# Retention and a Mish feed-forward layer on one core: the opening and the second block in another order

## The chip, the cores and the metric

The kernel runs on one core of one Trainium2 chip. The core has five engines with a queue of instructions each: TensorE (PE, with the loads of its stationary operand shown as PEld), VectorE (DVE), ScalarE (ACT), GpSimd (POOL) and SyncE (SP, which here only starts DMAs). They run side by side and wait for one another by semaphores. Matmuls write to PSUM, eight banks of 2 KB on each of 128 partitions; everything else lies in SBUF. The metric is the time of one execution on the device, in microseconds (us); lower is better.

## The reference

Two stages follow each other. The first is a recurrence over 768 positions for 4 batches and 8 heads of 64 elements, with one decay per head. Its output, 3072 rows of 512, goes through a two-layer feed-forward net whose middle is h * tanh(softplus(h)), the Mish function.

```python
batch, n_heads, seq, head_dim = (4, 8, 768, 64)
n_tokens, d_model, d_ff = (3072, 512, 2048)
for t in range(S):
    state = gamma[None, :, None, None] * state + np.einsum('bhd,bhe->bhde', k[:, :, t], v[:, :, t])
    y[:, :, t] = scale * np.einsum('bhd,bhde->bhe', q[:, :, t], state)
...
h = x @ w_in
sp = np.where(h > 20.0, h, np.log1p(np.exp(np.minimum(h, 20.0))))
g = h * np.tanh(sp)
return (g @ w_out).astype(np.float32)
```

## The kernel before

**The recurrence by chunks.** Positions are taken in 24 chunks of 128 (six to a batch). For a chunk the recurrence becomes matmuls: scores (k turned, times q turned), a triangular mask, the "present" product (masked scores times v), the outer product of k and v that updates the state, and the "past" product (the state before, times q). The decay is folded into q, k and v by tables (`qvs`) when they are cast to 16-bit floats. Two neighbouring chunks make a pair, numbered `n`; inside a pair, `m` is the first or second half of the positions, `a` the first or second four heads. For pairs 0 to 2 the functions are `cast_pair` (scale and cast), `turn_pair` (four transposes by TensorE into a PSUM tile `t_ps`, then a copy to SBUF), `pair_scores` (16 matmuls into a PSUM tile `at`, then one mask operation on DVE that gives `am`), `pair_outer` (into `u_ps`), `pair_state` (for m = 0 the middle state `mid`, for m = 1 `suh` and `sth`), `pair_present` and `pair_past` (both into `y_ps`) and `pair_xt` (copies y to `xt`, the input of the feed-forward net). Before `pair_past` adds to a y that `pair_present` has written, ScalarE copies one column of it to `seen`.

**The feed-forward net by blocks.** The first block is four chunks (512 rows), the others are two (256 rows). In a block, `g1` (line 560) multiplies weights with xt into `h_ps`, and ACT applies Mish (line 568). For block 0 a unit u of `g1` is four matmuls of 512 columns, 16 units in all; then come 16 units of the second layer (`g2_mm`, line 574), four matmuls each, the last two arranged so that output tiles end one after the other. The weights arrive as 32-bit floats in four slices for each layer, through staging tiles (`wstage`, four buffers), and are cast to 16 bit by `cast_win` (line 169, two halves to a slice, on DVE) and `cast_wout`. Later blocks do the second layer with seven products instead of eight (`seven`, line 660); nothing there is touched.

**The order.** It is written out by hand: within an engine the instructions run in the order in which the program issues them (`manual_schedule`). The function `first_block` (line 735) issues all loads on SP's queue in the order q, k, v of the first four chunks, first-layer weights, second-layer weights, the third pair; then it walks through the opening, lines 745 to 809. A dictionary `plan` (line 827) hangs further steps behind units of block 0: the casts of the second layer's weights, `turn_two` behind unit 24, the scores of pair 2 behind 25 and 26, `outer_two` behind 28 and `y_two` behind 30, which makes the input of block 1.

**PSUM.** Three tiles of a bank (`mm`), one of a bank (`px`) and two of two banks (`at`) share the eight banks, each group in rotation; a new tile waits until the readers of the one that it replaces are done. Two engines that access one PSUM tile are ordered by the program, also where they access different banks of it: in `turn_two`, the second eight transposes wait for the copy of the first eight, and of the two y in one tile the second is copied after the first.

**Identity matmuls.** `spin(n)` (line 378) multiplies the identity with itself, n times 128 columns, four at a time in one matmul of 512 columns, into a score tile that is overwritten afterwards. Its output is not used; it keeps TensorE busy where it would wait.

Of the kernel before, what the change touches and what calls it, by code (L numbers as in the profile page):

```python
# [10 lines left out]
FP32 = mybir.dt.float32  # L11
# [5 lines left out]
def kernel(  # L17
# [145 lines left out]

    def cast_win(s):
        src = wtmps.pop(("in", s))
        wins[s] = []
        for j in range(2):
            t = cpool.tile([P, NBP, TB // 2], FP16, name=f"win{s}_{j}")
            nc.vector.tensor_copy(t, src[:, :, j * (TB // 2):(j + 1) * (TB // 2)])
            wins[s].append(t)  # L170
# [27 lines left out]
    def turn_parts(parts, dst, on_act=False):  # L198
        t_ps = mmps.tile(list(dst.shape), FP16, name="t_ps", tag="mm")
        turn_into(parts, dst, t_ps, on_act)  # L200

    def turn_into(parts, dst, t_ps, on_act):
        for i in range(dst.shape[1]):
            for r in range(dst.shape[2]):
                nc.tensor.transpose(t_ps[:, i, r], parts(i, r), ident)  # L205
        if on_act:
            nc.scalar.copy(dst, t_ps)  # L207
        else:
            nc.vector.tensor_copy(dst, t_ps)
# [96 lines left out]
    def pair_state(n, u, m):  # L306
        g = 2 * n + m
        if m == 0:
            st = stp.tile([P, HP, D], FP16, name="mid")
            if n == 0:  # L310
                nc.vector.tensor_copy(st, u[0])
            else:
                nc.vector.tensor_tensor(st, u[0], states[g - 1], op=ALU.add)
# [63 lines left out]

    def spin(n):
        at = pairs[min(k for k in pairs if type(k) is tuple and k[1] == "at")]
        to = at.rearrange("p h i r c -> p h (i r) c")  # L380
        for i in range(0, n, HP):
            m = min(HP, n - i)
            nc.tensor.matmul(  # L383
                to[:, 0, :m], ident, ident.unsqueeze(1).broadcast_to((P, m, P)),
                start=True, stop=True)
# [349 lines left out]
    def first_block():  # L735
# [8 lines left out]

        pair_at(0, 0)
        spin(50)
        turn_first_q(qf, 0, True)
        spin(14)
        turn_first_q(qf, 1, False)
# [9 lines left out]
        turn_pair(0, "k", 0, True)  # L759
        spin(6)  # L760
        pair_scores(0, 0)
        pair_at(0, 1)
        spin(2)
        turn_pair(0, "k", 1, True)
        spin(6)
        pair_scores(0, 1)
        pair_at(1, 0)
        spin(2)
        turn_pair(1, "k", 0, True)
        spin(4)  # L770
# [36 lines left out]
        pair_state(1, u, 1)  # L807
# [11 lines left out]
        def turn_two():  # L819
            t_ps = atps.tile([P, 2, HP, 2, C], FP16, name="t_ps", tag="at")  # L820
            for j, nm in enumerate("qk"):
                pairs[2, nm + "t"] = qktp.tile([P, HP, 2, C], FP16, name="qkt", bufs=6)
                turn_into(
                    lambda i, r: pairs[2, nm, i // 2][:, r, i % 2 * 2:i % 2 * 2 + 2],
                    pairs[2, nm + "t"], t_ps[:, j], nm == "k")

# [34 lines left out]

    def banks(name, width):
        t = atps.tile([P, 2, TB], FP32, name=name, tag="at")
        return [t[:, m, :HP * width].rearrange("p (i c) -> p i c", i=HP) for m in range(2)]

    def outer_two():
        u = banks("u_ps", D)[:1]
        for a in range(2):
            pair_outer(2, u, a)
        pair_state(2, u, 0)  # L870

    def y_two():
        y = banks("y_ps", C)
        for a in range(2):
            pair_present(2, y, a)
        for m in range(2):
            nc.scalar.copy(seen, y[m][:, 0, :1])
# [120 lines left out]
```

## Time and profile before

| | |
|---|---|
| median of 3 runs | 212.36 us (210.85 to 212.54) |
| the profiled execution | 211.39 us, its span 209.6 us |
| mean granted TensorE clock | 0.984 |
| busy, share of the span | PE 94%, PEld 71%, DVE 52%, ACT 43%, POOL 35% |
| PE instructions | 2794 matmuls, 2794 weight loads |
| DMA | 38.75 MB, mean 185 GB/s |

Times in rows are counted from the first instruction of the span. A group of instructions is written as line, engine, operation, output <- inputs by the program's names, shapes and count, then busy time and the mean of one in ns, then the idle time of the engine just before and what ended it. A row of the timeline has start and length ahead of that. The chain is the work that ended last, followed back from the end; "issue" is time in which an engine waited for nothing that the profile shows. Line numbers are those of the kernel before.

### The profile page before, as it was taken

The numbers are of one execution on the slowest core, as the hardware profiler recorded it, in microseconds if no ns is written. First come the engines' busy times: TensorE is split into PE (matmuls) and PEld (weight loads), VectorE is DVE, ScalarE is ACT, GpSimd is POOL, SyncE is SP. The second block draws the span as 40 slices with busy tenths as digits, with TensorE's granted clock in tenths as the row PEclk, the third lists the DMA queues.
The fourth block names the chain that finished last, engine by engine and source line by source line (L and its number), as shares of the span: only waits on it lengthen the run. The fifth ranks groups of instructions, "written<-read, shape, count | busy, mean of one in ns | idle before, by whom it ended". The sixth has DMA issues, their size and how long they took to land.

```text
span 209.6 us, 6381 instructions
## 1 busy us (share of the span) xinstructions
PE 196.3 (94%) x2794; PEld 149.8 (71%) x2794; DVE 108.2 (52%) x195; ACT 89.7 (43%) x163; POOL 72.5 (35%) x91
## 2 busy tenths in 40 slices
PE   7973799998999999999999999999999999999994
PEld 2542244443486588888888888888788888888883
DVE  0583854005396445928765565745735734645062
ACT  2372266531154155254255254363364463452640
POOL 5550000738570500486551921913904800000000
PEclk9999599999999999999999999999999999999999
DMA  6999999999999995069999999999891430200202
GB/s 188 297 319 366 281 368 339 330 233 211 219 243 243 230 155 119 0 145 244 216 169 271 217 181 266 187 169 272 136 217 43 87 117 3 103 0 5 100 25 78
DMA packets 92828, 38.75 MB, mean 185 GB/s; under 512 B 76160, under 2 KB 86912, under 8 KB 92800
## 3 DMA queue, kind: packets, MB, share of 16 engines
q1 hardware_dynamic: 92656, 38.28, 82.5%
q8 instruction: 22, 0.36, 0.7%
q10 hardware_dynamic: 144, 0.05, 0.1%
q14 instruction: 6, 0.05, 0.1%
HBM read 27.32 MB, written 6.29 MB: 160 GB/s over the span
## 4 chain that ended last, share of the span: by engine, by line
PE 88%; ACT 4%; DMA 3%; issue 2%; DVE 1%; POOL 1%; SPq 0%; POOLq 0%; ACTq 0%; DVEq 0%
PE h_ps L560 41%; PE o_ps L660 27%; PE o_ps L574 9%; PE y_ps L493 4%; DMA kf<-in_k_dram 3%; ACT qkt L207 2%; PE at L405 1%; PE u_ps L412 1%; PE t_ps L205 1%; ACT xt L351 1%; PE y_ps L336 1%; PE at L282 1%; ACT v L248 1%; POOL qk L250 1%; PE y_ps L327 1%
## 5 line engine op out<-in xcount | busy, mean ns | idle before, releaser
L560 PE MATMUL h_ps<-xt,win 128*128 128x256 f16 (+1 forms) x704 | 88.3, 286 | 1.9 <-ACT xt L351 1.7
L560 PEld LDWEIGHTS <-win 128*128 128x128 f16 x704 | 68.9, 99 | 19.1 <-issue 3.6
L568 ACT ACTIVATE g<-h_ps 128x512 f16<-128x512 f32 x96 | 57.3, 597 | 50.9 <-PE h_ps L560 50.9
L660 PEld LDWEIGHTS <-gsum 128*128 128x128 f16 x288 | 27.0, 98 | 3.8 <-DVE gsum L638 0.4
L660 PE MATMUL o_ps<-tmat,gsum 128*128 128x256 f16 x216 | 26.4, 273 | 0.0
L360 POOL TENSOR_TENSOR qk<-qf,qvs 128x512 f16<-128x512 f32 x18 | 19.1, 1064 | 14.7 <-DMA qf<-in_q_dram 6.2
L660 PEld LDWEIGHTS <-g 128*128 128x128 f16 x216 | 21.1, 98 | 2.5
L574 PE MATMUL o_ps<-wout,g 128*128 128x512 f16 x96 | 22.4, 380 | 0.0
L364 POOL TENSOR_TENSOR v<-vf,qvs 128x512 f16<-128x512 f32 x18 | 20.6, 1145 | 1.6 <-DMA vf<-in_v_dram 1.5
L629 DVE TENSOR_TENSOR gsum<-g 128x512 f16<-128x512 f16 x18 | 7.9, 439 | 25.6 <-ACT g L568 25.6
L362 POOL TENSOR_TENSOR qk<-kf,qvs 128x512 f16<-128x512 f32 x18 | 20.3, 1125 | 0.2
L666 ACT COPY snap<-o_ps 128x256 f32<-128x256 f32 x27 | 10.1, 373 | 19.4 <-PE o_ps L660 19.4
L901 POOL COPY summed<-gsum 128x1 f16<-128x1 f16 x6 | 1.1, 188 | 48.6 <-DVE gsum L634 29.2
L660 PE MATMUL o_ps<-wout,g 128*128 128x256 f16 x144 | 17.2, 273 | 0.0
L674 DVE TENSOR_TENSOR osb<-o_ps,snap 128x256 f32<-128x256 f32 x27 | 11.4, 424 | 10.3 <-PE o_ps L660 5.9
L574 PEld LDWEIGHTS <-g 128*128 128x128 f16 x96 | 8.8, 98 | 9.7
L547 ACT CAST xt<-y_ps 128x512 f16<-128x512 f32 x13 | 7.2, 588 | 13.5 <-PE y_ps L493 13.5
L449 DVE TENSOR_TENSOR mid<-u_ps,sth 128x256 f16<-128x256 f32 x15 | 6.3, 422 | 11.3 <-PE u_ps L412 11.0
L482 DVE TENSOR_TENSOR am<-at,tri_half 128x1024 f16<-128x1024 f32 x9 | 10.9, 1214 | 0.0
L383 PE MATMUL at<-ident 128*128 128x512 f16 (+1 forms) x26 | 8.9, 470 | 1.4 <-POOL ident L96 1.4
L250 POOL TENSOR_TENSOR qk<-qf,qvs 128x512 f16<-128x512 f32 x2 | 2.1, 1076 | 23.0 <-PE h_ps L560 23.0
L660 PE MATMUL o_ps<-wout,gsum 128*128 128x256 f16 x72 | 9.4, 273 | 0.0
(77 smaller groups left out, 182.4 us busy)
## 6 DMA issues: line engine op xcount, KB each, us to landing
kf<-in_k_dram SPq DMA_DIRECT2D x24, 256.0 KB, 5.6
vf<-in_v_dram SPq DMA_DIRECT2D x24, 256.0 KB, 5.4
out_dram<-osb SPq DMA_DIRECT2D x22, 256.0 KB, 3.2
qf<-in_q_dram SPq DMA_DIRECT2D x20, 256.0 KB, 5.0
wt<-in_moe_w_out_dram SPq DMA_DIRECT2D x3, 1024.0 KB, 7.2
wi<-in_moe_w_in_dram SPq DMA_DIRECT2D x4, 512.0 KB, 7.7
wi<-in_moe_w_in_dram SPq DMA_DIRECT2D x2, 1024.0 KB, 11.2
qfirst<-in_q_dram SPq DMA_DIRECT2D x2, 512.0 KB, 4.5
```

Of the source, the lines that this page charges most:

```text
L360: nc.gpsimd.tensor_tensor(q16, qf, qs[g % 2].unsqueeze(2).broadcast_to((P, H, D)), op=ALU.mult)
L362: nc.gpsimd.tensor_tensor(k16, kf, boosts.unsqueeze(2).broadcast_to((P, H, D)), op=ALU.mult)
L364: nc.gpsimd.tensor_tensor(v16, vf, vs[g % 2].unsqueeze(2).broadcast_to((P, H, D)), op=ALU.mult)
L383: nc.tensor.matmul(to[:, 0, :m], ident, ident.unsqueeze(1).broadcast_to((P, m, P)), start=True, stop=True)
L482: nc.vector.tensor_tensor(am.rearrange("p a j i c -> p (a j i) c"), at.rearrange("p a j i c -> p (a j i) c"), tri_half.unsqueeze(1).broadc ...
L493: nc.tensor.matmul(ys[blk][s][half(hh), j, i], w, x, start=key not in begun, stop=True, skip_group_check=True)
L560: nc.tensor.matmul(h_ps[:, j], wins[s][f // 2][:, bp, f % 2 * P:(f % 2 + 1) * P], xts[blk][:, bp, :nt], start=(bp == 0), stop=(bp == NBP - 1))
L568: nc.scalar.activation(gt, h_ps, AF.Mish, scale=inv_boost3)
L574: nc.tensor.matmul(o_ps, gts[blk, fb][:, t * P:(t + 1) * P], wouts[s][:, f, cols], start=(fb == 0), stop=(fb == NFB - 1))
L660: nc.tensor.matmul(o_ps, x(f), w(f), start=first and f == 0, stop=f == n - 1, skip_group_check=True)
L666: nc.scalar.copy(x, o_ps)
L674: nc.vector.tensor_tensor(dst, o_ps, plus, op=ALU.add)
```

## The change

In the opening:

- The identity matmuls at its start and around the turns of pair 0 are issued with 128 columns each instead of 512 (`per=1`), 46, 14, 8 and 8 of them; the shorter runs after a new score tile go. Two of 512 and one of 512 columns stay ahead of the scores of pair 1.
- Both turns of pair 1 come ahead of its scores. The scaling of v stands behind these turns, and the outer product of pair 0 is split: four heads ahead of the last scores, four behind.
- The first middle state is copied by ACT instead of DVE. The second state of pair 0 is made behind its present product, and the outer product of pair 1 stands between present and past of pair 0.
- The y of pair 1 is two tiles of one bank (`mm`) instead of one tile of two banks (`at`). The copy of pair 0's second y is issued behind the `seen` copies of pair 1.
- The first half of the first weight slice is cast by POOL, ahead of the last two copies of y, instead of by DVE behind them.

At the end of block 0: `turn_two` makes all 16 transposes and then both copies on DVE; the present product of pair 2 gets a step of its own, one unit earlier than the past product; its y is two tiles, the first copied by DVE, the second by ACT.

```diff
-    def cast_win(s):
+    def cast_win(s, first_on=None):
...
-            nc.vector.tensor_copy(t, src[:, :, j * (TB // 2):(j + 1) * (TB // 2)])
+            (j == 0 and first_on or nc.vector).tensor_copy(
+                t, src[:, :, j * (TB // 2):(j + 1) * (TB // 2)])
...
     def turn_parts(parts, dst, on_act=False):
         t_ps = mmps.tile(list(dst.shape), FP16, name="t_ps", tag="mm")
-        turn_into(parts, dst, t_ps, on_act)
+        turn_only(parts, t_ps)
+        taken(dst, t_ps, on_act)
...
             if n == 0:
-                nc.vector.tensor_copy(st, u[0])
+                nc.scalar.copy(st, u[0])
...
-    def spin(n):
+    def spin(n, per=HP):
...
-        for i in range(0, n, HP):
-            m = min(HP, n - i)
+        for i in range(0, n, per):
+            m = min(per, n - i)
...
         pair_at(0, 0)
-        spin(50)
+        spin(46, 1)
         turn_first_q(qf, 0, True)
-        spin(14)
+        spin(14, 1)
         turn_first_q(qf, 1, False)
...
         turn_pair(0, "k", 0, True)
-        spin(6)
+        spin(8, 1)
         pair_scores(0, 0)
         pair_at(0, 1)
-        spin(2)
         turn_pair(0, "k", 1, True)
-        spin(6)
+        spin(8, 1)
         pair_scores(0, 1)
-        pair_at(1, 0)
-        spin(2)
         turn_pair(1, "k", 0, True)
-        spin(4)
         cast_pair(0, "v", 0)
-        pair_scores(1, 0)
-        pair_at(1, 1)
-        spin(2)
         turn_pair(1, "k", 1, True)
         for n, a in ((0, 1), (1, 0), (1, 1)):
             cast_pair(n, "v", a)
+        pair_at(1, 0)
+        spin(8)
+        pair_scores(1, 0)
+        u = [mmps.tile([P, HP, D], FP32, name="u_ps", tag="mm") for _ in range(2)]
+        pair_outer(0, u, 0)
+        pair_at(1, 1)
         spin(4)
         pair_scores(1, 1)
-        u = [mmps.tile([P, HP, D], FP32, name="u_ps", tag="mm") for _ in range(2)]
-        for a in range(2):
-            pair_outer(0, u, a)
-        for m in range(2):
-            pair_state(0, u, m)
+        pair_outer(0, u, 1)
+        pair_state(0, u, 0)
...
             pair_present(0, y, a)
+        nc.scalar.copy(seen, y[1][:, 0, :1])
         pair_xt(0, y, 0)
-        nc.scalar.copy(seen, y[1][:, 0, :1])
-        pair_past(0, y, 1)
-        pair_xt(0, y, 1)
-        u = banks("u_ps", D)
+        pair_state(0, u, 1)
+        u = u_banks()
         for a in range(2):
             pair_outer(1, u, a)
+        pair_past(0, y, 1)
         pair_state(1, u, 0)
-        y = banks("y_ps", C)
+        z = [mmps.tile([P, HP, C], FP32, name="y_ps", tag="mm") for _ in range(2)]
         for a in range(2):
-            pair_present(1, y, a)
+            pair_present(1, z, a)
         for m in range(2):
-            nc.scalar.copy(seen, y[m][:, 0, :1])
-        pair_past(1, y, 0)
-        pair_past(1, y, 1)
-        pair_xt(1, y, 0, False)
-        pair_xt(1, y, 1)
-        cast_win(0)
+            nc.scalar.copy(seen, z[m][:, 0, :1])
+        pair_xt(0, y, 1)
+        for m in range(2):
+            pair_past(1, z, m)
+        cast_win(0, nc.gpsimd)
+        pair_xt(1, z, 0, False)
+        pair_xt(1, z, 1)
         pair_state(1, u, 1)
...
             for j, nm in enumerate("qk"):
+                turn_only(
+                    lambda i, r: pairs[2, nm, i // 2][:, r, i % 2 * 2:i % 2 * 2 + 2], t_ps[:, j])
+            for j, nm in enumerate("qk"):
                 pairs[2, nm + "t"] = qktp.tile([P, HP, 2, C], FP16, name="qkt", bufs=6)
...
+                taken(pairs[2, nm + "t"], t_ps[:, j], False)
...
             29: [(outer_two,)],
+            30: [(present_two,)],
             31: [(y_two,)],
...
-    def y_two():
-        y = banks("y_ps", C)
+    def present_two():
+        y = pairs["y"] = [
+            atps.tile([P, HP, C], FP32, name="y_ps", tag="at") for _ in range(2)]
...
+    def y_two():
+        y = pairs["y"]
         for m in range(2):
             pair_past(2, y, m)
         for m in range(2):
-            pair_xt(2, y, m)
+            pair_xt(2, y, m, m == 1)
```

More of the change, by code (lines that the diff above doesn't have):

```diff
@@ L199, in turn_parts, with turn_only, taken @@
         t_ps = mmps.tile(list(dst.shape), FP16, name="t_ps", tag="mm")
-        turn_into(parts, dst, t_ps, on_act)
-    def turn_into(parts, dst, t_ps, on_act):
-        for i in range(dst.shape[1]):
-            for r in range(dst.shape[2]):
+        turn_only(parts, t_ps)
+        taken(dst, t_ps, on_act)
+    def turn_only(parts, t_ps):
+        for i in range(t_ps.shape[1]):
+            for r in range(t_ps.shape[2]):
                 nc.tensor.transpose(t_ps[:, i, r], parts(i, r), ident)
+    def taken(dst, t_ps, on_act):
         if on_act:
@@ L376, in cast_to @@
             ncast[0] += 1
-    def spin(n):
-        at = pairs[min(k for k in pairs if type(k) is tuple and k[1] == "at")]
+    def spin(n, per=HP):
+        at = pairs[min(x for x in pairs if type(x) is tuple and x[1] == "at")]
         to = at.rearrange("p h i r c -> p h (i r) c")
-        for i in range(0, n, HP):
-            m = min(HP, n - i)
+        for i in range(0, n, per):
+            m = min(per, n - i)
             nc.tensor.matmul(
@@ L821, in turn_two @@
             for j, nm in enumerate("qk"):
+                turn_only(
+                    lambda i, r: pairs[2, nm, i // 2][:, r, i % 2 * 2:i % 2 * 2 + 2], t_ps[:, j])
+            for j, nm in enumerate("qk"):
                 pairs[2, nm + "t"] = qktp.tile([P, HP, 2, C], FP16, name="qkt", bufs=6)
-                turn_into(
-                    lambda i, r: pairs[2, nm, i // 2][:, r, i % 2 * 2:i % 2 * 2 + 2],
-                    pairs[2, nm + "t"], t_ps[:, j], nm == "k")
+                taken(pairs[2, nm + "t"], t_ps[:, j], False)
         plan = {
@@ L860, in first_block, with u_banks @@
                 fn(*args)
-    def banks(name, width):
-        t = atps.tile([P, 2, TB], FP32, name=name, tag="at")
-        return [t[:, m, :HP * width].rearrange("p (i c) -> p i c", i=HP) for m in range(2)]
+    def u_banks():
+        t = atps.tile([P, 2, TB], FP32, name="u_ps", tag="at")
+        return [t[:, m, :HP * D].rearrange("p (i c) -> p i c", i=HP) for m in range(2)]
     def outer_two():
-        u = banks("u_ps", D)[:1]
+        u = u_banks()[:1]
         for a in range(2):
```

## The prediction

> **What bounds the kernel now.** I read the page first, then the chain that ended last in order of time over the first 60 us, then the busy times of the engines in 3.41 us windows with the granted clock.
>
> ```profile
> PE 88%; ACT 4%; DMA 3%; issue 2%; DVE 1%; POOL 1%; SPq 0%; POOLq 0%; ACTq 0%; DVEq 0%
> ```
>
> PE sets the time, so only stretches where PE stands still or runs slowly on this chain are worth anything. The chain shows them all in the opening and at the end of the first block:
>
> ```profile
> 16.94 2.36 issue
> 19.31 0.22 PE u_ps L300 x3
> ...
> 21.65 0.70 DVE xt L353
> 22.35 0.02 issue
> 22.37 0.59 ACT xt L351
> 22.97 0.04 issue
> 23.01 15.94 PE h_ps L560 x64
> 38.95 7.77 PE o_ps L574 x36
> ```
>
> (Start, length, what.) Two losses stand here. One is 2.36 us at 16.94 in the middle of an outer product whose last three matmuls wait for no data. The other is hidden in a busy row: 64 first-layer matmuls take 15.94 us, 0.249 each, while the 36 of the same width behind them take 7.77, 0.216 each. At 0.216 the 64 would take 13.8.
>
> The windows (length, busy of PE, PEld, DVE, ACT, POOL with counts, then granted clock, DMA share, GB/s) say why:
>
> ```profile
> 0.00:16.94 16.94, 13.04 (x223) 7.12 (x224) 8.93 (x11) 7.66 (x14) 8.87 (x27) 1.00 0.99 274
> 13.37:16.78 3.41, 2.15 (x121) 1.59 (x119) 2.98 (x4) 2.71 (x7) 0.17 (x1) 1.00 1.12 353
> 16.78:20.19 3.41, 0.83 (x52) 0.58 (x39) 0.85 (x2) 0.67 (x2) 0.00 (x0) 1.00 1.06 363
> 20.19:23.60 3.41, 1.65 (x18) 1.10 (x18) 1.95 (x4) 0.79 (x3) 0.00 (x0) 0.50 1.06 388
> 23.60:27.01 3.41, 3.41 (x10) 1.21 (x8) 3.38 (x7) 0.98 (x2) 0.00 (x0) 0.50 0.81 222
> 204.51:207.92 3.41, 1.96 (x18) 1.51 (x16) 1.27 (x3) 0.00 (x0) 0.00 (x0) 1.00 0.28 92
> q8 instruction: 22, 0.36, 0.7%
> q8 instruction: 1, 0.02, 5.7%
> ```
>
> A window with PE busy for 0.83 of 3.41 us (24%), the one with the stop, is followed by half clock. It goes on through one of 48% and ends with one that is full. Windows at 63% and 57% (the first row with a length of 3.41 and the last) cost no clock. The two lines below are the DMA queue of code, first over the whole span, then between 16.5 and 17.7 us: one packet of 0.02 MB, the first of this queue in the span. It lands inside the stop, and 223 + 224 = 447 PE instructions lie before the stop. So I read the stop as PE out of code: the first 447 were there, the next block came late because the DMA share is 0.99 up to there.
>
> **The change, part by part.** I laid out the new order instruction by instruction with the durations of these rows (groups have busy time and mean ns, timeline rows start and length; the line on landing is that of `wi`):
>
> ```profile
> 7.39 4.15 POOL L250 TENSOR_TENSOR qk<-kf,qvs 128x512 f16<-128x512 f32 x4 [3.33 <-DMA kf<-in_k_dram]
> L207 ACT COPY qkt<-t_ps 128x512 f16<-128x512 f16 x4 | 2.3, 586 | 3.0 <-PE t_ps L205 3.0
> L666 ACT COPY snap<-o_ps 128x256 f32<-128x256 f32 x27 | 10.1, 373 | 19.4 <-PE o_ps L660 19.4
> L209 DVE COPY qkt<-t_ps 128x1024 f16<-128x1024 f16 x2 | 1.4, 691 | 11.4 <-PE t_ps L205 11.4
> 24.25 3.69 DVE L169 CAST win<-wi 128x1024 f16<-128x1024 f32 x6
> 9.01 6.00 SPq L152 DMA_DIRECT2D wi<-in_moe_w_in_dram  x6
> DMA to landing us min/median/max: 6.0/8.8/11.2
> L318 DVE TENSOR_TENSOR sth<-suh,gch 128x256 f16<-128x256 f32 x2 | 0.8, 424 | 0.1
> 9.61 0.42 PE L282 MATMUL at<-qkt 64*64 64x128 f16 x16 [0.35 <-ACT qkt L207]
> 12.68 0.42 PE L282 MATMUL at<-qkt 64*64 64x128 f16 x16 [0.46 <-ACT qkt L207]
> 14.05 1.67 ACT L248 ACTIVATE v<-vf 128x512 f16<-128x512 f32 x3
> ```
>
> *Shorter identity matmuls.* 26 matmuls become 79 of nearly the same columns (90 to 88 times 128). No time is saved: the chain here runs over the landing of k (POOL waits 3.3 us for it). But each is two PE instructions, so the opening has 106 instructions more, and 176 stand before the first scores instead of 78. PE's code is fetched by blocks: 22 packets move 0.36 MB, about 16 KB, or 256 instructions each, by the 5588 instructions of PE and PEld. If the late block is asked for one block ahead, that is at instruction 447 - 256 = 191: before, in the third scores, at 12.68; after (counting two per matmul) in the first scores, at 9.61. The latency was 19.31 - 12.68 = 6.6 us, so the code is there at 16.2. PE then comes to instruction 447 in the middle of the first "present" product, at 14.6. The stop is 1.6 us instead of 2.36. Bounds: no stop at all (a fetch 1.6 us faster), and, if what is queued ahead on the DMA sets the landing and not the request, 17.8: the first weight load, issued before the request, lands at 9.0 + 6.0 = 15.0 (row above), and PE went on at most 19.31 - 16.5 = 2.8 after the code packet began.
>
> *Turns ahead of scores, v behind the turns.* The fourth k cast still ends at 11.5. ACT now runs copy, v, copy and then the three v casts from 11.8: 0.59 + 0.56 + 0.59 + 1.67 = 15.2, where it ended at 15.7 before. The first mid moves from DVE to ACT's end (0.37, by the snap row), so the state chain on DVE begins at 15.5 and ends at 16.5, 0.7 earlier. DVE's masks end before that.
>
> *Outer between present and past, y in two tiles.* After the code arrives at 16.2: rest of present 0 and outer 1 to 17.2 (16 and 32 matmuls by the 0.42 for 16 of the score rows, readable 0.2 later), mid 17.7, present 1 to 17.85, two reads of `seen` to 18.25, the past products to 18.5. Before, DVE's copy of the first y waited for both past products and ACT's for DVE's copy (0.70, then 0.59 in the chain), since both halves were one tile. As two tiles they run side by side; but ACT has also the delayed copy of y 1 (0.59) ahead of its own, so it ends at 18.25 + 0.59 + 0.59 = 19.4. DVE: the second half of the first weight slice at 17.7 (3.69 / 6, 0.62), then its copy, 18.5 to 19.2. The first layer starts at **19.45** instead of 23.01: **3.55 us**.
>
> *The first weight cast on POOL.* The rows hold no POOL cast of 128x1024. Bounds: DVE's 0.62, and twice POOL's two-input 128x512 (4.15 / 4), 2.1; I take 2.1, the same engine. The weight lands at 15.0; POOL has done its masks by then, so the cast ends at 17.1, two us ahead of its use. Behind it on POOL stand only the casts of the second block, whose loads come much later. SP is the other side: its first second-layer load waits for both casts of this slice and is now released some five us earlier, but on the DMA, full then, it stands behind the first-layer loads. Nothing of this is counted.
>
> POOL's cast runs beside DVE's `sth`. What two such do to each other shows here, both started near 59 us:
>
> ```profile
> 58.92 0.68 DVE L613 TENSOR_TENSOR tmat<-wout 128x1024 f16<-128x1024 f16 x1
> 59.64 1.42 DVE L614 TENSOR_TENSOR tmat<-wout,tmat 128x1024 f16<-128x1024 f16 x1
> 59.08 1.43 POOL L360 TENSOR_TENSOR qk<-qf,qvs 128x512 f16<-128x512 f32 x1 [2.21 <-DMA qf<-in_q_dram]
> ```
>
> The same DVE shape takes 0.68 alone and 1.42 beside POOL, and POOL 1.43 instead of 1.04. So `sth` could end at 17.55 instead of 16.5. With the stop at 16.2 the `seen` reads at 18.25 cover this, and DVE is 0.25 later, 19.45, level with ACT. Without the stop it would cost 0.9. The Trainium skill, "SBUF — State Buffer", section "SBUF: two separate sides", says of the port pair that VectorE and GpSimd share that a VectorE operation with two SBUF inputs and a GpSimd read lock each other out for a whole instruction. By that rule the loss is as just worked out, and the rows agree.
>
> *Clock.* With the start at 19.45 PE's poorest 3.41 us has, by this layout, some 1.7 to 1.9 us busy (49% to 56%). Kept were 57% and 63%, lost 24%. I take it as kept: 64 matmuls at 0.216, 13.8 instead of 15.94, **2.1 us**. The Trainium skill, "TensorE: Matmul & The Clock Gate", Part 1 (The HAM clock gate), gives an activity window of about 3.4 us and half rate after an idle one; the 6.8 us at 0.50 are two such windows, though here a window 24% busy sufficed.
>
> *Second block.* PE's own rows:
>
> ```profile
> 47.95 0.61 PE L205 MATMUL t_ps<-ident,qk 128*128 128x128 f16 x8 [0.78 <-DVE qkt L209]
> 49.66 0.42 PE L282 MATMUL at<-qkt 64*64 64x128 f16 x16 [0.24 <-ACT qkt L207]
> 56.51 0.41 PE L336 MATMUL y_ps<-qkt,sth 64*64 64x128 f16 x8 [0.51 <-ACT seen L877]
> 58.30 1.91 PE L560 MATMUL h_ps<-xt,win 128*128 128x256 f16 x16 [0.19 <-ACT xt L351]
> ```
>
> 1.72 us of idleness. Sixteen transposes in a row remove the 0.78, but both copies (0.69 each on DVE) then follow them, and only four matmuls lie beside: about 0.8 idle at the scores instead of 1.02. The `seen` wait (0.51) falls under four matmuls. DVE, however, must first finish two output copies (128x512 from PSUM, as the 0.70 of its xt) before its copy of y, so the next block waits some 0.5 instead of 0.19. Together **0.4 us**, between 0 and 1.2.
>
> *What is late next.* PE would now come six us earlier to all that the DMA brings:
>
> ```profile
> 29.22 1.23 DVE L179 CAST wout<-wt 128x2048 f16<-128x2048 f32 x1 [1.27 <-DMA wt<-in_moe_w_out_dram]
> 39.48 1.14 ACT L248 ACTIVATE qk<-kf 128x512 f16<-128x512 f32 x2
> 43.72 1.05 ACT L177 CAST wout<-wt 128x1024 f16<-128x1024 f32 x1 [0.46 <-DMA wt<-in_moe_w_out_dram]
> ```
>
> Even at these old times all are ready. The third weight slice (the third and fourth of the six casts from 24.25) is half cast by 26.1 and needed at 19.45 + 32 x 0.216 = 26.4; the second layer's first by 30.5, needed at 33.2; k of the second block by 40.6, needed at 41.0; the last quarter by 44.8, needed at 48. Two margins are under half a us, so a start earlier than 19.45 gains little more.
>
> **The sum**: 3.55 + 2.1 + 0.4 = 6.05 us. The profiled execution took 211.39 (span 209.6 and 1.79 around it), so 205.3 for it; the median of the runs is 0.97 above that execution, so **206.3** beside 212.36.
>
> **Rivals.** *The clock halves all the same* (25%). For it: 49% to 56% lies under the lowest share seen kept, and the window's phase may differ. Half clock from about 17 us to 23.6 costs 0.5 in the products and half of 3.6 in the first layer, 2.3: 208.6. To 27 us it costs 4: 210.3.
>
> *The code comes no earlier than the DMA lets it* (10%). All loads issued up to the request are served first; then it is there at 17.8, the start is 1.6 later, 21.05, and the clock falls as before: 1.95 + 0.4, 210.0.
>
> *The stop is not code* (5%), and 2.4 us of it stay, with the half clock: without the 1.6 at present 0 the start is near 20.9, gain 2.1 + 0.4, 209.9. Against it stand the packet inside the stop and the absence of a wait. The Trainium skill, "Runtime: NRT & Kernel Launch", section Instruction fetch mechanics, says so in effect: 16 KiB blocks, whose fetch is mostly hidden, and room for 2048 instructions on PE. The block size agrees with the trace; the hiding and the room do not, with a stop at 447.
>
> *Slower* (8%): POOL's cast, and DVE locked beside it. Its place is between 15.0 and the first layer; nothing else can supply that weight. It decides once it ends after about 23 us, that is when it lasts over 8 us, four times my price, because PE then idles and loses its clock as well. At 10 us the first layer starts at 25.05 and loses 1.7 more by half clock: 40.6 at its end instead of 38.95, less 0.4: 213.6.
>
> **How the numbers follow.** 52% for the forecast, which spreads from 204 (no stop: one us more at most) to 208 (the second block gives nothing, or the stop is a us longer). With the halved clock and half of the two 210 cases, the range is 204 to 210.3. Faster by over 1% (about what a measurement here can tell from no change) means under 210.2: 80%; within 1%: 12%, from the ends of the 210 cases; slower: 8%.
>
> **What would show it.** Right: first h_ps at 19 to 20 us; an "issue" row of 1 to 2 us inside L327's group instead of L300's; no 0.50 in the windows; no wait of ACT xt for DVE xt. Wrong: granted clock of 0.50 between 17 and 27; POOL's weight cast over 4 us; PE waiting for DVE win or wout past 25 us; a second code stop some 25 matmuls into the first layer.

## The result and the profile after

The changed kernel takes 204.13 us (median of four, 203.94 to 206.89) beside 211.84 us for the kernel before (median of four, 210.85 to 212.54). The ratio is 0.967, with a 95% interval of 0.958 to 0.976. The forecast was 206.3 us.

The profiled execution took 203.98 us with a span of 202.2 and a mean TensorE clock of 0.998. The chain that ended last, of the kernel after, in order of time (start, length, what), for the stretch that the prediction is about:

```profile
7.89 6.96 DMA vf<-in_v_dram
...
14.87 0.64 ACT v L252
...
17.17 0.65 PE y_ps L340 x16
...
17.84 0.59 ACT xt L355
...
18.48 0.69 DVE xt L357
19.18 0.14 issue
19.32 13.97 PE h_ps L564 x64
33.29 7.77 PE o_ps L578 x36
...
41.99 1.30 DVE qkt L213 x2
...
43.33 0.42 PE at L286 x16
...
50.34 0.97 PE o_ps L578 x4
...
51.33 3.77 PE h_ps L564 x33
```

Three things are to be seen. The first layer starts at 19.32 where it started at 23.01, and the row of 2.36 us of "issue" has no successor: the longest such row here is 0.14. The 64 matmuls of the first layer take 13.97 instead of 15.94. From their end to the next block's first matmul there are 18.04 us (33.29 to 51.33) instead of 19.35 (38.95 to 58.30). What the chain starts from is new as well: the load of v, which landed at 14.85.

The windows of 3.41 us of the kernel after (length; busy of PE, PEld, DVE, ACT, POOL with counts; granted clock, DMA share, GB/s) are laid from the first change of clock in the trace (6.96 us), so that a change falls on an edge. They keep full clock through the poorest one, in which PE is busy for 1.91 us, 56%:

```profile
17.20:20.62 3.42, 1.91 (x23) 1.07 (x23) 2.73 (x6) 1.43 (x4) 0.45 (x1) 1.00 1.08 369
20.62:24.03 3.41, 3.41 (x17) 1.54 (x16) 1.23 (x2) 2.35 (x5) 0.00 (x0) 1.00 1.05 387
```

The timeline of the same execution shows who releases whom ahead of the first layer and at the end of the block (start, length, engine and line, idle time before and what ended it):

```profile
14.87 0.63 ACT L252 ACTIVATE v<-vf 128x512 f16<-128x512 f32 x1 [0.43 <-DMA vf<-in_v_dram]
16.47 1.18 POOL L169 CAST win<-wi 128x1024 f16<-128x1024 f32 x1 [2.94 <-DMA wi<-in_moe_w_in_dram]
16.32 0.43 DVE L322 TENSOR_TENSOR sth<-suh,gch 128x256 f16<-128x256 f32 x1
17.88 0.69 DVE L169 CAST win<-wi 128x1024 f16<-128x1024 f32 x1 [0.60 <-DMA wi<-in_moe_w_in_dram]
49.39 1.29 DVE L587 COPY osb<-o_ps 128x512 f32<-128x512 f32 x2 [1.65 <-PE o_ps L578]
50.38 0.58 ACT L355 CAST xt<-y_ps 128x512 f16<-128x512 f32 x1 [1.13 <-PE y_ps L340]
50.59 0.68 DVE L357 CAST xt<-y_ps 128x512 f16<-128x512 f32 x1
```

Three engines wait for the DMA here, which they did not do before: ACT for the last v, POOL for the first half of the weight slice (landed near 16.4, before at 15.0), DVE for the second half (near 17.85). The code queue carried its first packet early, as the DMA view of the kernel after between 11.8 and 13.1 us shows:

```profile
q8 instruction: 1, 0.02, 5.8%
```

The packet runs from 11.82 to 13.04; before, from 16.59 to 17.68. Where the 7.41 us between the two profiled executions (211.39 and 203.98) came from:

| place | before | after | gain | forecast |
|---|---|---|---|---|
| first layer starts | 23.01 | 19.32 | 3.69 | 3.55 |
| its 64 matmuls | 15.94 | 13.97 | 1.97 | 2.1 |
| from there to the next block | 19.35 | 18.04 | 1.31 | 0.4 |
| the rest | | | 0.44 | 0 |

The rest lies behind the start of the next block and is not followed further.

### The profile page after: what moved, and what is told of

The parts are those of the page before. It is cut to its first block, busy times and chain, and to the rows that moved or that the text cites. A ratio compares the mean times of both kernels' runs of the same rounds, so it can differ in the third digit from the quotient of the medians.

```text
span 202.2 us, 6489 instructions
## 1 busy us (share of the span) xinstructions
PE 194.1 (96%) x2847; PEld 153.3 (76%) x2847; DVE 110.0 (54%) x195; ACT 88.6 (44%) x162; POOL 73.4 (36%) x92
## 4 chain that ended last, share of the span: by engine, by line
PE 89%; DMA 3%; SPq 3%; DVE 1%; ACT 1%; issue 0%
PE h_ps L564 42%; PE o_ps L664 28%; PE o_ps L578 10%; PE y_ps L497 4%; DMA vf<-in_v_dram 3%; SPq L236 3%; PE at L409 1%; PE u_ps L416 1%; PE y_ps L340 1%; DVE qkt L213 1%; PE y_ps L331 1%; SPq L194 0%; PE t_ps L207 0%; PE at L286 0%; DVE xt L357 0%
## 5 line engine op out<-in xcount | busy, mean ns | idle before, releaser
L564 PE MATMUL h_ps<-xt,win 128*128 128x256 f16 (+1 forms) x704 | 86.2, 282 | 1.5 <-DVE xt L357 1.5
L364 POOL TENSOR_TENSOR qk<-qf,qvs 128x512 f16<-128x512 f32 x18 | 18.7, 1041 | 17.4 <-DMA qf<-in_q_dram 17.4
L387 PE MATMUL at<-ident 128*128 128x128 f16 (+1 forms) x79 | 8.2, 278 | 1.4 <-POOL ident L96 1.4
L664 PE MATMUL o_ps<-tmat,g 128*128 128x256 f16 x72 | 9.3, 273 | 0.0
```

The costliest lines, as they stand in the source:

```text
L364: nc.gpsimd.tensor_tensor(q16, qf, qs[g % 2].unsqueeze(2).broadcast_to((P, H, D)), op=ALU.mult)
L387: nc.tensor.matmul(to[:, 0, :m], ident, ident.unsqueeze(1).broadcast_to((P, m, P)), start=True, stop=True)
L564: nc.tensor.matmul(h_ps[:, j], wins[s][f // 2][:, bp, f % 2 * P:(f % 2 + 1) * P], xts[blk][:, bp, :nt], start=(bp == 0), stop=(bp == NBP - 1))
L664: nc.tensor.matmul(o_ps, x(f), w(f), start=first and f == 0, stop=f == n - 1, skip_group_check=True)
```

## The experiments

The theory after the result: the narrow identity matmuls bring the first code block about five us earlier, so the stop goes, and with it the half clock; the rest of the opening, and the second block apart from it, give about two us. The rival: the new order of the opening did it, and the width of the identity matmuls is of no account. Each ratio is to the kernel before on the same chip.

### The new order with wide identity matmuls

```diff
-        spin(46, 1)
+        spin(46)
...
-        spin(14, 1)
+        spin(14)
...
-        spin(8, 1)
+        spin(8)
...
-        spin(8, 1)
+        spin(8)
```

> The changed kernel with its identity matmuls 512 columns wide again (46, 14, 8 and 8 times 128 columns as before, in matmuls of up to 512), all else as changed. Theory 'code': the late block of PE code is asked for some 4 us later, its packet comes at 15.5 to 17 us instead of 11.8, PE stops for 1.5 to 3 us at the second present product, the clock falls to 0.50 behind it, the first layer starts at 21 to 22 us; 3 to 5 us slower than the changed kernel, 207 to 209. Rival 'order': the new order of turns, scores and products removed the stop; then within 0.5 us of the changed kernel, about 204. Second expectation of 'code': the load under way when the packet runs is the one that lands late; so the last v lands at 13.5 again instead of 14.85, and the first weight at 15.0.

Measured: 210.0 us (209.31 to 210.81), ratio to the kernel before 0.989 [0.985, 0.993]. The chain of this kernel has the stop again, and longer:

```profile
15.71 0.41 PE y_ps L340 x8
16.13 3.44 issue
19.56 0.69 PE y_ps L331 x32
...
22.24 16.36 PE h_ps L564 x64
```

PE stands for 3.44 us after its 449th instruction, at the place where it stood before after 449 too (447 matmuls and weight loads, the count of the prediction, and two instructions at 0.3 and 0.7 us that only synchronise). The packet begins at 16.96 and PE goes on at 19.56. The half clock follows (from 20.28 to 27.11), and the first layer takes 16.36. The loads behave as expected too: the last v lands at 13.88, 0.89 behind the one ahead of it, the first weight half at 15.37, and the one that lands late is a later weight load (19.57, 2.68 behind the one ahead of it at 16.89). The rest of the change is in this kernel, and it is worth 1.1%; the width is the remaining 2.2%. The rival falls.

### The old order with narrow identity matmuls

```diff
-        spin(50)
+        spin(50, 1)
...
-        spin(14)
+        spin(14, 1)
...
-        spin(6)
+        spin(6, 1)
...
-        spin(6)
+        spin(6, 1)
```

> The kernel before with nothing changed but the width of the identity matmuls (50, 14, 6 and 6 of 128 columns each). Theory 'code': no stop of 2.36 us, no half clock, first layer at 20 to 20.5 us; 4 to 5 us faster than before, about 207. Rival 'order': no change, within 1 us of before.

Measured: 207.61 us (206.87 to 208.51), ratio 0.978 [0.973, 0.983]. The width alone takes 2.2% off the kernel before, the same 2.2% by which its absence fell short in the last one: the two parts add (1.1 and 2.2 make the 3.3 of the whole change). The chain has no stop, and the first layer starts at 20.67:

```profile
17.36 0.25 PE u_ps L300 x20
17.61 0.48 PE y_ps L327 x32
...
19.31 0.70 DVE xt L353
...
20.03 0.59 ACT xt L351
...
20.67 15.66 PE h_ps L560 x64
```

Here ACT's copy waits for DVE's, as before; the two tiles for y take that away (see the kernel with one tile below). One window of this execution ran at half clock (15.66 in place of 13.97); of its four executions two show a mean clock of 1.000 and 206.87 us, two show 0.992 and 208.3 to 208.5. So one half-clock window in the first layer costs 1.5 to 1.6 us in whole executions, beside 1.69 in the row.

### The second block undone

```diff
                 pairs[2, nm + "t"] = qktp.tile([P, HP, 2, C], FP16, name="qkt", bufs=6)
+                taken(pairs[2, nm + "t"], t_ps[:, j], nm == "k")
...
-            30: [(present_two,)],
...
-    def present_two():
-        y = pairs["y"] = [
-            atps.tile([P, HP, C], FP32, name="y_ps", tag="at") for _ in range(2)]
+    def y_two():
+        t = atps.tile([P, 2, TB], FP32, name="y_ps", tag="at")
...
-            pair_xt(2, y, m, m == 1)
+            pair_xt(2, y, m)
```

> The changed kernel with the second block's steps of before (copy of q on DVE between the two turns, copy of k on ACT, present and past products in one step, y in one tile, both copies on ACT). Theory: the second block is worth what the two traces differ by from the end of the first layer to the first matmul of the next block (19.35 against 18.04): 1.3 us slower than the changed kernel, 205.4. Rival, the forecast's 0.4: 204.5.

Measured: 207.56 us (207.05 to 208.46), ratio 0.978 [0.974, 0.982]. The chain of this kernel:

```profile
20.03 15.66 PE h_ps L564 x64
35.69 7.77 PE o_ps L578 x36
...
53.92 1.08 ACT xt L355 x2
...
55.04 7.04 PE h_ps L564 x63
```

35.69 to 55.04 is 19.35, to the hundredth what the kernel before has, beside 18.04 after: the second block is worth 1.31 us. The whole difference of 3.4 us to the changed kernel is larger. The profiled execution has a span 3.9 us longer; beside the 1.31, 0.71 is a later start (20.03) and 1.69 a half-clock window, neither of which the edit touches. The later start comes from the loads: the first q lands 0.5 us later than in the changed kernel and the last v 0.72 later (15.57). One execution with a clock of 1.000 took 207.05. The changed kernel's executions at that clock took 203.9 to 205.8 in its two groups of runs, 1.2 to 3.1 us less. So the 1.31 is read from the traces; whole executions do not give it as sharply, and what lies beyond it stays open.

### The second weight half behind the copy of y

```diff
-        cast_win(0, nc.gpsimd)
+        cast_win(0, nc.gpsimd, (0,))
         pair_xt(1, z, 0, False)
+        cast_win(0, None, (1,))
```

> The changed kernel with the second half of the first weight slice cast on DVE behind the copy of y instead of ahead of it. Theory: the first layer waits for DVE, which waited for this half to land (17.85) ahead of its copy; with the copy first it starts at 18.5 instead of 19.32, and the half is cast by 19.3, ahead of its use at 20.2: 0.6 to 0.8 us faster than the changed kernel, 203.4. Rival: the weights' landing sets the time anyway, or ACT's two copies end as late: less than 0.2 us.

(The last copy of y, by DVE, now goes ahead of the second half of the first weight slice.) Measured: 204.31 us (204.05 to 204.93), ratio 0.963 [0.960, 0.966]. Its chain:

```profile
17.95 0.59 ACT xt L356
...
18.63 13.97 PE h_ps L565 x64
```

and the same view around 124 us:

```profile
119.88 4.21 DMA qkt<-qk
...
124.14 0.22 PE at L410 x2
```

The first layer starts 0.69 us earlier than in the changed kernel, and the next block 0.69 earlier too (50.64). But the span is 202.3: the gain is given back at 124 us, where PE waits 0.65 us for a score matmul whose transposed q and k come by DMA. That wait shows in the changed kernel's second profile (below) and not in its first. DVE's weight cast is what the changed kernel's start waits for, not ACT's three copies.

### The gap filled, and the changed kernel again

In the first of these, three identity matmuls of 512 columns go into PE's gap ahead of the first layer, on top of the last edit:

```diff
+        pair_at(9, 0)
+        spin(12)
+        del pairs[9, "at", 0]
+        cast_win(0, nc.gpsimd, (0,))
```

> The changed kernel with the second half of the first weight cast behind the copy of y, and three identity matmuls of 512 columns (into a score tile of their own) in the gap between the past products and the first layer. So far the clock fell after 3.41 us windows with PE busy for 25%, 19%, 42% and 48%, and held after 56% and more; the changed kernel's poorest window was 56%. Theory: this gap decides in some executions whether the first layer's first 3.4 us run at half clock, 1.7 us; filled, no execution shows it, the runs lie together within 1 us, and the median is 0.5 to 1 us below the changed kernel on the same chip. Rival: the clock is no matter of the gap, or the time comes back later at a DMA; then the same spread and median.

The second is the changed kernel itself.

> The changed kernel itself once more, to stand beside the runs of this call. Theory: most executions at about 204, some 1.7 to 3 us above, where the clock fell once behind the wait for xt.

Measured on one chip, six executions each: 204.37 us (203.86 to 205.37), ratio 0.963 [0.960, 0.966], with the fill; 205.55 us (204.17 to 206.88), ratio 0.969 [0.964, 0.974], for the changed kernel. The intervals touch, so a version that beats the changed kernel is not shown; what differs is the upper end. Two of the changed kernel's six executions, 206.78 and 206.88, have a mean clock of 0.992 and 0.991, and the slowest of its first four had 0.990; none with the fill is under 0.999. Its executions lie within 1.5 us of each other, where 1 was expected. The chain of the changed kernel's second profile, around 125 us, has the DMA wait:

```profile
120.67 4.63 DMA qkt<-qk
...
125.34 0.22 PE at L409 x2
```

PE stood 1.11 us for it, and this execution, at full clock and with the first layer at 19.38, took 205.26, 1.28 us more than the first profiled one. With the fill the first layer started at 19.55, later and not earlier, because of DVE:

```profile
16.60 1.21 DVE L323 TENSOR_TENSOR sth<-suh,gch 128x256 f16<-128x256 f32 x1
```

This is the row that took 0.43 at 16.32 in the changed kernel. POOL's cast began at 16.48 here, ahead of it, and lasted 1.04 (more on this in the last section).

### The weight cast back on DVE

```diff
-        cast_win(0, nc.gpsimd)
+        cast_win(0)
```

> The changed kernel with both halves of the first weight slice cast on DVE at the same place. The first half landed at 16.34 in the changed kernel, the second at 17.85, and DVE was free from 17.27. Theory: DVE casts the first half while it waits for the second, so the first layer starts at the same 19.3 and the move to POOL is worth nothing. Rival, that POOL frees DVE: 0.6 us later.

Measured: 206.68 us in one execution, with a half-clock window (the first layer takes 15.53) and a DMA wait of 1.0 us near 126, which make up nearly all of the 2.7 us above the changed kernel's profile. The part that answers the question is on DVE's timeline:

```profile
17.28 1.39 DVE L169 CAST win<-wi 128x1024 f16<-128x1024 f32 x2
18.59 0.68 DVE L357 CAST xt<-y_ps 128x512 f16<-128x512 f32 x1
```

Both halves are done at 18.67 and the first layer starts at 19.32, as in the changed kernel. The second half lands near 17.9 in both (17.85 and 17.95), and DVE casts the first half while it waits. Moving the cast to POOL was worth nothing here.

### One tile for y of pair 1

```diff
-        z = [mmps.tile([P, HP, C], FP32, name="y_ps", tag="mm") for _ in range(2)]
+        t = atps.tile([P, 2, TB], FP32, name="y_ps", tag="at")
+        z = [t[:, m, :HP * C].rearrange("p (i c) -> p i c", i=HP) for m in range(2)]
```

> The changed kernel with the y of pair 1 in one tile of two banks again (first block only). Theory: DVE's copy waits for both past products and ACT's copy for DVE's, so ACT's ends some 0.6 us behind DVE's and the first layer starts at 19.9 instead of 19.3. Rival: two tiles bring nothing here, since DVE's copy is held up by the weight anyway; 19.3.

Measured: 206.36 us in one execution, with one half-clock window. The chain:

```profile
18.67 0.69 DVE xt L357
...
19.38 0.59 ACT xt L355
...
20.02 15.36 PE h_ps L564 x64
```

ACT's copy follows DVE's again and the start is 20.02 instead of 19.32. Of these 0.70 us, 0.19 belong to the second weight half, which lands at 18.04 here instead of 17.85 and moves DVE's copy from 18.48 to 18.67. The two tiles are worth the other 0.5 us.

### Only the first run of identity matmuls narrow

```diff
-        spin(14, 1)
+        spin(14)
...
-        spin(8, 1)
+        spin(8)
...
-        spin(8, 1)
+        spin(8)
```

> The changed kernel with only the first run of identity matmuls narrow (46 of 128 columns); the runs of 14, 8 and 8 are 512 wide again, so PE has 44 instructions less in the opening, and instruction 449 moves into the outer product of pair 1. Two readings of when the late code is asked for. 'At issue': with instruction 193, now in the second scores at 11.0, and the packet starts some 3.8 us later, 14.8, PE stops for about 2 us at 15.5, and the load under way at 15 us (the first weight half) lands late. 'Ahead': up to 64 instructions earlier, while PE waits for the k cast at 8 to 9 us; the packet starts at 12 to 13, no stop.

Measured: 210.75 us in one execution. The code packet begins at 13.29 and there is no stop, so the first 46 narrow matmuls suffice. That bears on where the block is asked for. The prediction had it at instruction 191. Counted from the execution of that instruction, the packet begins 1.22 us later here, 2.14 in the changed kernel, 3.78 before and 4.05 with the wide matmuls. Counted from instruction 129 it is 4.39, 4.34, 5.44 and 5.55, and over all fourteen traces 4.0 to 5.6, where 191 gives 1.2 to 4.1. But 129 is not singled out: from instruction 80 the delays are 6.4 to 7.9, a spread as narrow. So the first block is asked for well ahead of 191; from which instruction, the traces do not tell. The second block is different: its packet begins 3.6 to 4.2 us after instruction 450, the first one of the block that came just before it, in all fourteen traces; there one block ahead is what they show.

The time itself has other causes: two half-clock windows (from 19.43 and from 128.66), 1.79 us of waiting for the DMA transposes near 126 us, and 1.21 us of "issue" at 145.13. That last one is a code stop too, far from the opening: PE stands after its instruction 4033, which is 449 and 14 times 256, and a packet of the code queue runs from 143.61 to 144.89.

### What work keeps the clock

The forecast read the clock as following PE's busy share. The kernel just told speaks against that. Its windows:

```profile
16.02:19.43 3.41, 2.21 (x82) 1.51 (x72) 3.20 (x6) 2.19 (x7) 1.04 (x1) 1.00 1.10 353
19.43:22.84 3.41, 3.17 (x8) 1.19 (x9) 2.09 (x5) 0.60 (x1) 0.00 (x0) 0.50 1.05 384
```

65% busy, and half clock follows. In the changed kernel's second profile a window of 48% was not followed by it:

```profile
16.96:20.37 3.41, 1.63 (x21) 0.98 (x21) 2.76 (x6) 1.39 (x4) 0.73 (x1) 1.00 1.08 362
20.37:23.78 3.41, 3.41 (x18) 1.56 (x16) 0.95 (x2) 2.39 (x4) 0.00 (x0) 1.00 1.05 387
```

What differs is the kind of work: the 65% were all matmuls on 64x64 quarters of the array. The busy share alone does not decide either: in the kernel with the second block undone the window from 17.20, also at 48% (1.65 of 3.42 us), was followed by half clock. By columns times the part of the array they use, lost windows have at most 31% (this one 25%), kept ones at least 34%; in the opening alone it is 30% and 38%. Two kernels tested that reading: on top of the edit that puts DVE's copy of y first, 40 matmuls in the gap, on a quarter of the array in the first and on all of it in the second, each 512 columns.

```diff
+        pair_at(9, 0)
+        hold = pairs.pop((9, "at", 0)).rearrange("p h i r c -> p h (i r) c")
+        for _ in range(40):
+            nc.tensor.matmul(
+                hold[:D, 0, :HP], ident[:D, :D],
+                ident[:D].unsqueeze(1).broadcast_to((D, HP, P)), start=True, stop=True)
```

> The kernel with the copy of y first, and in the gap ahead of the first layer 40 identity matmuls of 512 columns on a 64x64 quarter of the array, one behind the other (added work, some 8.6 us at full clock). PE is busy all through. By 'share of time busy' the clock holds: 0.216 us each, first layer at about 26.5. By 'work in the array' (columns times the part of the array that they use, over what the whole array could take in 3.41 us: clock lost at 30% and less, kept at 38% and more in the runs so far) these are 25%, so the clock falls after the first window that they fill, at 21 to 25 us, and the matmuls behind it take 0.427 us.

> The same 40 matmuls on the whole array. By both readings the clock holds; 0.216 us each, first layer at about 26.5. Stands beside the quarter ones.

Measured: 212.69 us and 212.11 us, both at full clock throughout. The windows with the quarters:

```profile
19.66:23.07 3.41, 3.41 (x17) 1.71 (x16) 1.56 (x3) 0.00 (x0) 0.00 (x0) 1.00 1.04 382
23.07:26.48 3.41, 3.41 (x17) 1.50 (x14) 1.36 (x3) 0.00 (x0) 0.00 (x0) 1.00 1.07 393
```

These windows use 25% and 23% of the array's capacity and keep the clock, so that reading falls too. One that fits the windows of these kernels was formed only afterwards: the share of time in which columns stream, where four quarter products that run side by side count once and a lone one counts in full. It gives at most 31% for the lost windows, 34% and more for the kept ones, and about 100% for these two. The profile's busy share would overstate the small matmuls then, whose ends it models. It was not tested, and the criterion stays open.

### Half as wide again

```diff
-        spin(46, 1)
+        spin(6, 1)
+        at = pairs[0, "at", 0].rearrange("p h i r c -> p h (i r) c")
+        for _ in range(80):
+            nc.tensor.matmul(at[:, 0, 0, :D], ident, ident[:, :D], start=True, stop=True)
```

> The changed kernel with its first run of identity matmuls as 6 of 128 and 80 of 64 columns, the same columns in 40 matmuls more (80 PE instructions). The late code is asked for earlier still. Theory: its packet starts near 9 to 10.5 us instead of 11.8, and the load under way then (v's first or second) is the one that lands a us or so late, while the last of v and the weights land as late as in the changed kernel, not earlier; no stop; first layer at about 19.3 all the same. Rival: the late landing of v at 14.85 has nothing to do with the packet and stays where it is.

Measured: 210.01 us in one execution. The code packet begins at 10.14, in the window expected. The second v, then under way, lands at 13.20 (2.35 us behind the first, where they follow each other by 0.9 otherwise), but the last v is there at 14.97 and the weight halves at 16.48 and 17.98, 0.12 to 0.14 later than in the changed kernel: an earlier packet moves the delay to an earlier load, and the loads behind it stay as late. That there would be no stop and a first layer at 19.3 did not come true. PE's timeline shows why:

```profile
16.22 0.81 PE L331 MATMUL y_ps<-am,v 64*64 64x128 f16 x31
19.90 0.64 PE L340 MATMUL y_ps<-qkt,sth 64*64 64x128 f16 x8 [2.87 <-issue]
```

A stop of 2.87 us after instruction 705, that is 256 after 449, with the second code packet at 17.33. The first layer starts at 21.64, half clock runs from 19.41 to 26.24, and PE waits another 1.3 us for the DMA transposes near 130. More instructions in the opening bring the first block earlier and also bring PE to the end of the second before that is there.

## Why the forecast held, and where its working did not

**The stop is code: shown.** With the wide matmuls the stop after 449 instructions is there in either order, with the narrow ones in neither, and the first code packet of the span lies inside the stop, or it ends at least 1.3 us ahead of the first instruction that needs it. The stops come after 449 instructions (twice), after 705 and after 4033, all a multiple of 256 apart, each with a code packet inside. The Trainium skill, "Runtime: NRT & Kernel Launch", section Instruction fetch mechanics, gives blocks of 16 KiB: the packets' size and the 256 instructions between 449 and 705 agree. It has the fetch mostly hidden and room for 2048 instructions on PE; stops of 2.36, 3.44, 2.87 and 1.21 us say otherwise here.

**"The stop is 1.6 us instead of 2.36": wrong.** The step that failed is "asked for one block ahead, that is at instruction 191", with its latency of 6.6 us. The packet came 4.77 us earlier (11.82 instead of 16.59), not 3.1, and nothing was left of the stop. For the first packet the request lies further ahead than one block; one block ahead fits only the second packet. The announced sign, an "issue" row of 1 to 2 us in L327's group, did not come.

**Loads at their old times: wrong.** The prediction kept the loads as they were. The early packet falls among the loads of v, and the one under way ends late: the last v at 14.85 (2.24 behind the one ahead of it, 12.61) and both weight halves 1.33 later than before. In the kernel before the packet held up the next weight load instead, 16.52 to 19.54, when nobody needed it yet. The two errors offset each other, 1.6 us of stop that did not come and 1.33 us of load that was not foreseen. That the start of 19.45 was off by only 0.13 is therefore luck. The path to the start was another: the last v (ACT at 15.51), then the second weight half (17.85), DVE's cast and copy.

**The clock: right in its size, not in its criterion.** The 64 matmuls gave 1.97 where 2.1 was said. The Trainium skill, "TensorE: Matmul & The Clock Gate", Part 1 (The HAM clock gate), lets the half rate follow an idle window; here it followed windows with PE busy up to 65%. That the clock "halves all the same" got 25%; of ten executions of the changed kernel three show a mean clock of 0.990 to 0.992, at 206.8 to 206.9 us. The windows begin at another time in each execution (the first change of clock lies between 4.2 and 7.4 us in the traces). That this decides whether the half clock comes is likely: with the copy of y first (four executions) and with the fill (six), which leave a shorter gap or none, it did not come. It was not shown by itself.

**Where the 2.2 us below the forecast come from.** 0.91 are the second block, 0.44 the rest of the table, and 0.82 the scatter of executions: the forecast put the median 0.97 above the profiled execution, and after the change it lies 0.15 above. Start and clock nearly cancel.

**Second block, "0.4 us, between 0 and 1.2": too small, 1.31.** The two copies after sixteen transposes cost 0.52 us of idleness where 0.8 was counted. That they overlap (1.30 for both, not 1.38) is the smaller part of it: 1.38 less the four matmuls beside them, at 0.216, leaves 0.52 already, so the 0.8 was mis-sized. Above all the term for DVE failed: its copy of y was to be late by 0.5. DVE's row of the two output copies ends at 50.68, that of y (the two overlap by 0.09) runs from 50.59 to 51.27, and PE ends its own work at 51.31: just hidden.

**POOL's cast: between the bounds, 1.18 us.** The price taken was 2.1, with two-input rows for a one-input cast. It is off the path either way: with the cast on DVE the start was the same 19.32. The rival in which POOL makes the kernel slower had no ground at this price.

**What is late next.** The weights and the second block's loads were ready, as listed. What the list missed lies later: the DMA transposes of q and k at 124 to 133 us, for which PE waits 0.65 to 1.79 us in seven of these traces. This bounds what a still earlier start can give.

## What to carry to other kernels

Where an engine stands still without waiting for data, look at the queue of code packets and count the instructions up to the stop: filler instructions that cost nothing in time still move the point at which the next block is asked for, and too many bring the next stop. A packet or load that comes earlier on a full DMA makes another one later; write down which. Before an early gain is counted in full, ask which later wait is nearly on the path already, and try it with a kernel that only brings the start forward.

## What the runs showed of the hardware

- **Code.** Packets of 16 KB, of which the first two of an execution take 1.05 to 1.2 us each; PE goes on 1.4 to 1.6 us after the end of one that it stood for (17.68 to 19.31 before the change, 18.12 to 19.56 with wide matmuls in the new order, 18.45 to 19.90 in the last kernel, 144.89 to 146.34 with one narrow run). In the changed kernel PE comes to instruction 450 at 14.38, 1.3 us after the packet's end, and does not stop; the margin is small.
- **A code packet among loads.** In all fourteen traces a load lands late by 0.3 to 1.5 us against the usual spacing, in twelve by over 0.8; it is the one under way when the first packet comes, and in the kernel with one narrow run the one behind it. Which mechanism does it the traces do not show.
- **DVE and POOL.** In the changed kernel the state product `sth` starts at 16.32 and POOL's cast at 16.47: `sth` takes 0.43 and the cast 1.18. With the fill the cast starts first (16.48, 1.04 long), and `sth`, begun at 16.60, ends at 17.81, 0.29 after the cast. With only the first run narrow it is the same: cast 16.48, `sth` from 16.84 to 17.80, and with the wide matmuls too: cast 15.49, `sth` from 16.16 to 16.81. In all three `sth` ends 0.28 to 0.29 us after the cast, whenever it began: who is first goes through, and the other is held. In the changed kernel `sth` was first by 0.15 us. The prediction allowed for one us here; 0.2 to 0.8 was paid in these three kernels and nothing in the changed one. The Trainium skill, "SBUF — State Buffer", section "SBUF: two separate sides", says that of a VectorE operation with two SBUF inputs, as `sth` is, and a GpSimd one that reads SBUF, whoever starts first keeps the port pair for the whole instruction; the traces agree. A version with DVE's copy ahead of the second weight half and POOL's cast taken away was not tried.
